# Dealing 256 KB of a weight matrix to the eight lower DMA engines of a load-bound decode kernel

## Chip, cores and metric

One core of one Trainium2 chip. The metric is the device time of one execution, in microseconds (us). The profile is one execution recorded by the hardware profiler; its span is some 2 us shorter than the time of the same execution (658.6 against 660.69 for the kernel before).

## The reference

```python
xn = _layernorm(x)                      # x: 2 x 1 x 512, bf16
q  = (xn @ wq) -> 2 x 32 x 1 x 128
scores = q k_cache^T * 128**-0.5        # k_cache, v_cache: 2 x 32 x 8192 x 128
attention = softmax(scores) @ v_cache -> @ wo      # wo: 4096 x 512
mlp = relu(xn @ w1) @ w2                # w1: 512 x 1792, w2: 1792 x 512
return x + attention + mlp
```

Nearly all of the 280.5 MB that are read are keys and values. w2, which the change touches, is 1.8 MB.

## The kernel before

SyncE issues every large load into one queue, in the order in which the data is needed: wq, w1, w2, then key and value tiles of 4 MB, at the end wo in five pieces. A 128-partition load is carried by all sixteen DMA engines (the trace has sixteen landings for each), so each load is complete only when its slowest engine is. w2 goes 14 rows of 1 KB to a partition:

```python
w2_sb = w_sb[:, KT*Dff : KT*Dff + FT*D].rearrange("p (j n) -> p j n", j=FT)   # FT = 14
...
@(lambda f: f(nc.sync))
def _(sp):
    sp.dma_start(w1_sb, B_w1.rearrange("(p kt) f -> p kt f", kt=KT)).then_inc(dW1, 16)
    sp.dma_start(w2_sb, B_w2.rearrange("(p j) n -> p j n", j=FT)).then_inc(dW2, 16)
    load_k(0); load_k(1); load_v(0)
    for t in range(NP - 2):                   # NP = 32 pairs of heads
        sp.wait_ge(pT[NG - 1], t + 1);  load_k(t + R)
        sp.wait_ge(sW, t + 1);          load_v(t + 1)
    ...                                       # last values in two halves
    for c in range(NC):                       # wo, cuts (0, 14, 21, 27, 30, 32)
        sp.dma_start(wo_sb[:, sl, :], wo_v[:, sl, :]).then_inc(dW[c], 16)
```

TensorE does the MLP while the first keys are on their way, and then loops over the pairs:

```python
    for j in range(FT):                       # 14 x 4 products of w1
        for kt in range(KT): pe.matmul(hp[:, j, :], lhsT=w1_v[:, kt, j, :], rhs=xz[...], ...)
    ...
    pe.wait_ge(sF, 2); pe.wait_ge(dW2, 16)    # ReLU done (VectorE), w2 landed
    for j in range(FT):                       # 14 products of w2
        pe.matmul(y, lhsT=hT[:, j, :], rhs=w2_sb[:, j, :], ...)
    ...
    with pe.Fori(16, 16 * (NP // R) + 1, 16) as n16:      # 16 turns of R = 2 pairs
        for r in range(R): pe.reg_add(reg, reg, 1); step(r, reg, n16)
```

## Time and profile before

| | before |
|---|---|
| time, 3 runs | 660.98, 663.39, 1773.56 us (median 663.39) |
| profiled execution | 660.69 us, span 658.6 |
| DMA engines busy with data (mean of sixteen) | 99.2% of the span |
| TensorE busy | 85% |
| last piece of wo lands on eight engines / on the other eight | 653.04 to 653.44 / 654.67 to 654.85 us |

The last row says that half of the engines finish 1.4 us later than the other half, although nothing shows that they carry more bytes: the 128 packets of w2 (0.537 us each) land on all sixteen within 0.38 us, which is less than one packet.

Two groups of instructions show which side waits for which. In a line of this view stand the source line, the engine, what is done, the count, then busy time and mean ns of one, then the engine's idle time just before these instructions and what ended it.

```profile
L285 PE MATMUL tp<-identb,ks 128*128 128x128 bf16 x4096 | 323.5, 229 | 68.4 <-DMA ks<-in_A_k_cache_dram 68.4
...
L305 PE MATMUL ot<-prm,vs 128*128 128x64 bf16 x4224 | 156.1, 192 | 4.2 <-issue 4.2
```

TensorE idles 68.4 us ahead of the transposes of keys, all of it for key loads; "issue" (time in which the profile shows nothing that the engine waited for) is 4.2 us ahead of the value products.

The packets show directly what makes an engine late. The first of the instruction blocks (nine packets of 16 KB, on a queue of their own) runs from 29.574 to 30.634 us. Two engines end a data packet at 29.578. Behind one of them the data goes on at once; behind the other the next data packet begins only at 30.620 and takes 1.68 us, where the others take 1.21.

### The profile page before, as it was taken

How to read it: one execution, taken by the hardware profiler on the slowest of the kernel's cores; microseconds unless marked ns; L12 is line 12 of the kernel's file. 1: busy time of each engine (PE TensorE's matmuls, PEld its weight loads, DVE VectorE, ACT ScalarE, POOL GpSimd, SP SyncE). 2: the span in 40 equal slices, each digit the busy share in tenths (PEclk: the TensorE clock that was granted, in tenths of full speed). 3: DMA queues.
4: the chain of work that ended last, by engine and by line, in shares of the span. 5: the costliest groups of instructions: out<-in, count | busy, mean ns of one | idle time of the engine just before them, and what ended most of it. 6: DMA issues, size and time to landing. Idle time of an engine off the chain costs nothing.

```text
span 658.6 us, 26859 instructions
## 1 busy us (share of the span) xinstructions
PE 559.9 (85%) x12737; PEld 535.1 (81%) x12737; DVE 253.2 (38%) x436; ACT 255.8 (39%) x403; POOL 9.0 (1%) x46
## 2 busy tenths in 40 slices
PE   2998799987989878879887887997878997887896
PEld 0488798987879878879887887987878987887895
DVE  1144344442434433334443343443434443333441
ACT  1043444443433434334353434344333444333340
POOL 1000000000000000000000000000000000000000
PEclk9799999998998988999898899898989998898988
DMA  8999999999999999999999999999999999999996
GB/s 365 430 444 418 439 430 429 432 428 442 422 442 424 436 428 432 432 428 444 420 442 428 432 430 430 434 430 442 424 436 428 432 432 428 440 424 442 426 424 281
DMA packets 10542, 280.66 MB, mean 426 GB/s; under 512 B 1186, under 2 KB 1188, under 8 KB 1700
## 3 DMA queue, kind: packets, MB, share of 16 engines
q1 hardware_dynamic: 10528, 280.50, 99.2%
q8 instruction: 9, 0.15, 0.1%
q14 instruction: 1, 0.01, 0.0%
q10 hardware_dynamic: 4, 0.00, 0.0%
HBM read 280.50 MB, written 0.00 MB: 426 GB/s over the span
## 4 chain that ended last, share of the span: by engine, by line
DMA 58%; PE 37%; ACT 2%; issue 1%; SPq 1%; ACTq 0%; DVE 0%
DMA ks<-in_A_k_cache_dram 54%; PE tp L285 21%; PE Sc L292 11%; PE ot L305 4%; DMA w_sb<-in_A_wo_dram 4%; ACT kT L412 2%; ACT L412 1%; SPq L187 0%; PE Sc L340 0%; SPq L182 0%; PE Sc L343 0%; SPq L170 0%; SPq L169 0%; SPq L163 0%; PE ot L397 0%
## 5 line engine op out<-in xcount | busy, mean ns | idle before, releaser
L285 PE MATMUL tp<-identb,ks 128*128 128x128 bf16 x4096 | 323.5, 229 | 68.4 <-DMA ks<-in_A_k_cache_dram 68.4
L412 DVE COPY kT<-tp 128x1024 bf16<-128x1024 bf16 x320 | 219.7, 691 | 324.3 <-PE tp L285 324.2
L285 PEld LDWEIGHTS tp<-identb,ks 128*128 128x128 bf16 x4096 | 254.8, 102 | 72.3 <-DMA ks<-in_A_k_cache_dram 72.2
L412 ACT COPY kT<-tp 128x1024 bf16<-128x1024 bf16 x192 | 194.3, 1012 | 233.4 <-PE tp L285 233.3
L292 PE MATMUL Sc<-q,kT 128*128 128x64 bf16 x4096 | 216.8, 196 | 7.6 <-ACT kT L412 5.7
L292 PEld LDWEIGHTS Sc<-q,kT 128*128 128x128 bf16 x4096 | 178.4, 100 | 11.3 <-ACT kT L412 9.0
L305 PE MATMUL ot<-prm,vs 128*128 128x64 bf16 x4224 | 156.1, 192 | 4.2 <-issue 4.2
L305 PEld LDWEIGHTS ot<-prm,vs 128*128 128x128 bf16 x4224 | 139.0, 97 | 7.0 <-issue 4.4
L525 ACT COPY nm<-Sc 128x2 f32<-128x2 f32 x32 | 5.1, 160 | 118.5 <-PE Sc L343 118.5
L529 ACT ACTIVATE prm<-Sc,nm 64x128 bf16<-64x128 f32 x64 | 25.7, 401 | 4.3
L466 DVE TENSOR_REDUCE mcol<-Sc 64x1 bf16<-64x128 f32 x64 | 18.6, 290 | 18.7 <-PE Sc L292 18.3
L412 ACT ACT_TABLE_LOAD x16 | 20.5, 1283 | 2.2
L240 PE MATMUL ot<-vs,xz 128*16 128x512 bf16 x32 | 9.5, 470 | 8.6 <-DMA vs<-in_A_wq_dram 8.6
L517 ACT COPY OTf<-ot 128x2 f32 x32 | 5.1, 160 | 26.9 <-PE ot L305 26.9
L471 DVE TENSOR_REDUCE mx<-Sc 1x2 bf16<-1x128 bf16 x32 | 8.9, 278 | 16.9 <-PE Sc L340 16.9
L240 PEld LDWEIGHTS ot<-vs,xz 128*16 128x16 bf16 x32 | 3.3, 105 | 14.4 <-issue 12.2
L225 POOL COPY q<-qb 128x2 bf16<-128x2 bf16 x32 | 5.8, 184 | 588.9 <-PE Sc L292 566.1
L529 ACT ACTIVATION_READ_ACCUMULATOR prm<-Sc,nm x64 | 11.8, 185 | 0.0
L442 DVE TENSOR_SCALAR qs<-ot 16x512 bf16<-16x512 f32 x1 | 0.7, 679 | 18.0 <-PE ot L240 18.0
L340 PE MATMUL Sc<-identb,mcol 128*1 128x128 bf16 x32 | 7.0, 217 | 0.0
L270 PE MATMUL Sc<-w_sb,hT 128*2 128x512 bf16 x14 | 5.8, 604 | 0.1
L343 PE MATMUL Sc<-mx,onesb 1*128 1x2 bf16 x32 | 5.5, 172 | 0.0
(56 smaller groups left out, 37.5 us busy)
## 6 DMA issues: line engine op xcount, KB each, us to landing
ks<-in_A_k_cache_dram SPq DMA_DIRECT2D x32, 4096.0 KB, 26.7
vs<-in_A_v_cache_dram SPq DMA_DIRECT2D x31, 4096.0 KB, 31.3
vs<-in_A_wq_dram SPq DMA_DIRECT2D x1, 4096.0 KB, 12.1
vs<-in_A_v_cache_dram SPq DMA_DIRECT2D x2, 2048.0 KB, 19.3
w_sb<-in_B_w_dram SPq DMA_DIRECT2D x2, 1792.0 KB, 17.9
w_sb<-in_A_wo_dram SPq DMA_DIRECT2D x1, 1792.0 KB, 25.4
w_sb<-in_A_wo_dram SPq DMA_DIRECT2D x1, 896.0 KB, 27.1
w_sb<-in_A_wo_dram SPq DMA_DIRECT2D x1, 768.0 KB, 28.5
```

Of the source, the lines that this page charges most:

```text
L225: g.tensor_copy(q2[t % R][:], qb[:, 2 * t:2 * t + 2]).then_inc(sQ1, 1)
L240: i = pe.matmul(qp, lhsT=xz[:, kt, Z - g * Bsz:Z - g * Bsz + QG * Bsz], rhs=vs[1][:, (kt * QG + g) * 512:(kt * QG + g + 1) * 512], start=( ...
L270: i = pe.matmul(y, lhsT=hT[:, j, :], rhs=w2_sb[:, j, :], start=(j == 0), stop=(j == FT - 1),)
L285: t = pe.transpose(tp[e % 4][:, i, :], ks[r][:, kk * Dh:(kk + 1) * Dh], identb[:])
L292: t = pe.matmul(Sc[r][:, 2 * kk:2 * kk + 2 * REP], lhsT=kT[e % 4][:, i, :], rhs=rep(q2[r][:]), start=True, stop=True,)
L305: t = pe.matmul(ot[r][:, 0:2 * REP], lhsT=vs[r][:, kk * Dh:(kk + 1) * Dh], rhs=rep(prm[r][:, kk, :]), start=(kk == 0), stop=(kk == KB - 1),)
L340: pe.transpose(tr_of(r), mcol[r][:], identb[:]).then_inc(sT, 1)
L343: pe.matmul(bc_of(r), lhsT=onesb[:], rhs=mx[r][:], start=True, stop=True).then_inc(sB, 1)
L412: fn(kT[e % 4][:], tp[e % 4][:]).then_inc(kR[e], 1)
L466: m = v.tensor_reduce(out=mcol[i][half, :], in_=S_of(i)[half, :, u], axis=AX.X, op=ALU.max)
L471: v.tensor_reduce(out=mx[i][:], in_=tr_of(i).rearrange("o (u m) -> o u m", u=2), axis=AX.X, op=ALU.max, negate=True,).then_inc(sX, 1)
L529: x = a.activation(out=prm[i][half, :, u], in_=S_of(i)[half, :, u], func=ACTF.Exp, bias=nm[i][half, u:u + 1], scale=1.0, accum_out=RS[half ...
```

## The change

The intent: give every partition 12 rows of w2 in one load, and send the other 256 rows, 4 to a partition, to the lower 64 partitions only. They come in eight loads of 8 rows. Each takes every fourth partition, p, p+4 ... p+28. That such a load goes to a fixed half of the DMA engines was my assumption; the trace of after bears it out (64 landings for the eight loads, and two clusters in the first keys, below). I call the eight that take the small loads the lower ones, engines 0 to 7, and the others the upper ones, 8 to 15; these are names, for the trace has no numbers. An upper engine then carries 16 KB less (eight packets of 12 KB in place of 14), a lower one 16 KB more (the same, and eight of 4 KB). The MLP's products follow the new layout. Cut to its core:

```diff
+    FA = FT - 2               # 12 rows on all partitions
+    FB = 2 * (FT - FA)        # 4 more on the lower 64
+    FJ = FA + FB              # 16
...
-        sp.dma_start(w2_sb, B_w2.rearrange("(p j) n -> p j n", j=FT)).then_inc(dW2, 16)
+        sp.dma_start(
+            w2_sb[:, 0:FA, :], B_w2[0:P * FA, :].rearrange("(p j) n -> p j n", j=FA)
+        ).then_inc(dW2, 16)
+        w2_v = B_w2[P * FA:, :].rearrange("(p j) n -> p j n", j=FB)
+        for p in (0, 1, 2, 3, 32, 33, 34, 35):
+            sl = slice(p, p + 29, 4)
+            sp.dma_start(w2_sb[sl, FA:FA + FB, :], w2_v[sl]).then_inc(dW2b, 16)
...
-        for j in range(FT):
+        for j in range(FJ):                       # products of w1: 48 + 16 of half width
             for kt in range(KT):
                 i = pe.matmul(
-                    hp[:, j, :],
-                    lhsT=w1_v[:, kt, j, :],
+                    hp[0:HP if j >= FA else P, j, :],
+                    lhsT=w1_b[:, kt, j - FA, :] if j >= FA else w1_a[:, kt, j, :],
...
+        pe.wait_ge(dW2b, 16 * 8)
-        for j in range(FT):
+        for j in range(FJ):                       # 12 products of w2, and 4 over 64 partitions
...
-        v.tensor_scalar(out=hT[:], in0=hp, ..., op0=ALU.max).then_inc(sF, 1)
+        for sl in (slice(0, P), slice(0, FA)), (slice(0, HP), slice(FA, FJ)):
+            t = v.tensor_scalar(out=hT[sl], in0=hp[sl], ..., op0=ALU.max)
+        t.then_inc(sF, 1)
```

## The prediction

> **What bounds the kernel now.** I read the page first: busy shares, the queue lines, then the chain that ended last.

> ```profile
> span 658.6 us, 26859 instructions
> ...
> DMA  8999999999999999999999999999999999999996
> ...
> q1 hardware_dynamic: 10528, 280.50, 99.2%
> q8 instruction: 9, 0.15, 0.1%
> ...
> DMA 58%; PE 37%; ACT 2%; issue 1%; SPq 1%; ACTq 0%; DVE 0%
> ```

> The transfers are the bound: the data queue's packets fill 99.2% of sixteen DMA engines' span, while TensorE, the busiest compute engine, is at 85%. The next question is whether the queue ever runs dry. The view by stretch of time says no: the DMA share (the column before GB/s) is 1.00 in every stretch until the last loads.

> ```profile
> 2.00:33.00 31.00, 19.51 (x114) 8.94 (x115) 3.62 (x9) 2.46 (x4) 2.22 (x9) 0.89 1.00 421
> 33.00:159.00 126.00, 110.68 (x2702) 107.31 (x2698) 53.84 (x92) 54.95 (x87) 1.29 (x7) 1.00 1.01 432
> 159.00:623.00 464.00, 401.99 (x9264) 392.49 (x9264) 185.69 (x312) 190.42 (x299) 4.24 (x23) 0.94 1.00 432
> ```

> So the end is set by bytes per DMA engine plus whatever else an engine is made to do. The chain of waits, in order of time, shows how it closes: the output weights' last piece lands, then a short tail.

> ```profile
> 625.73 29.12 DMA w_sb<-in_A_wo_dram
> 654.85 0.05 issue
> 654.90 0.39 PE ot L397 x8
> ```

> A load is complete when its last engine is, so I read the sixteen landings of every load in the trace one by one. w2 lands between 21.28 and 21.66 us, all sixteen within 0.38. The first key tile already has one straggler: fifteen between 31.01 and 31.39, one at 32.73. In the tile that lands from 108.70 on, seven are late; the last piece of wo lands on eight engines at 653.04 to 653.44 and on eight at 654.67 to 654.85. The cause stands in the packets of the queue named "instruction": seven 16 KB blocks between 29.57 and 107.2 us and one at 650.36 (the ninth, at 654.27, comes too late to matter), 1.07 us each on average. After every one of them exactly one more engine is about 1.3 us late and stays so. No engine is hit twice before the end. The kernel therefore ends some 1.4 us after its eight unhindered engines are done (654.85 against 653.44), with no difference in the bytes they carry.

> [...]

> **The change part by part.** Its only aim can be that deal: 256 KB of w2 (64 partitions x 4 rows x 1 KB) ride on engines 0 to 7, and engines 8 to 15 are relieved of 2 rows in each of 8 partitions, 16 KB.

> Upper engines: w2's 14336-byte packets take 0.537 us each, 8 of them 4.29 (first landings of w1 and w2 are 17.00 and 21.28, which agrees). With 12 rows I estimate 12/14 x 0.537 = 0.460, times 8 = 3.68: 0.61 us less.

> Lower engines: the same 3.68, plus eight 4 KB packets. From 3072 bytes in 0.122 us and 6144 in 0.241 I put 4 KB at 0.161, plus 0.009 for each load's semaphore write: 8 x 0.170 = 1.36. In all 5.04 against 4.29: 0.75 us more.

> If the eight late engines are the upper ones, their last landing goes from 654.85 to 654.24, and the lower ones' from 653.44 to 654.19: evened out almost exactly, 0.6 us gained. That is all there is to win here.

> Beside that, SyncE issues eight more loads ahead of the first keys. The two neighbours take 0.42 us to issue, so the first key tile is issued about 8 x 0.47 = 3.8 us later, near 6.1 us. The queue then holds work until 21 us: hidden.

> TensorE and VectorE pay too:

> ```profile
> 22.70 3.52 PE L253 MATMUL ot<-xz,w_sb 128*128 128x2 bf16 x56
> ...
> 26.26 0.19 DVE L446 TENSOR_SCALAR hT<-ot 128x28 bf16<-128x28 f32 x1 [2.77 <-PE ot L253]
> ...
> 26.50 5.84 PE L270 MATMUL Sc<-w_sb,hT 128*2 128x512 bf16 x14
> ...
> 32.77 1.51 PE L285 MATMUL tp<-identb,ks 128*128 128x128 bf16 x24 [0.43 <-DMA ks<-in_A_k_cache_dram]
> ```

> 56 products of w1 become 48 plus 16 of half width: at 3.52/56 = 0.063 us each, 8 more are 0.50. The second ReLU adds about 0.2. w2's 14 products become 16; they follow each other every 0.43 us, so 0.85 more. w2 has landed by about 22.8 on the slower engines, before this block needs it. Sum 1.55 us, less the 0.43 of waiting in the last line: TensorE starts on the first keys 1.1 us later. Does that starve the queue? I took, for each load, its time of issue against the first landing of the load before it. The smallest margin in the loop is 5.3 us (the key tile issued at 83.61; what stood before it began to land at 89.28), and 15 to 20 us after 190 us, once TensorE waits for keys. So 1.1 us is swallowed, and a change that lengthens a compute chain still costs nothing.

> Sum on the path to the end: 0.6 us less of 658.6, 0.1%.

> **The rivals.** First, the late engines are not the upper ones. The refills take a new engine each time, which looks like going round in order, but nothing in this trace says where the round begins. If one late engine is among the lower eight, the end moves from 654.85 to about 655.6, +0.75 us. For it: the lack of engine numbers. Against it: the change only makes sense if its author saw the slack in the lower half[...]. I give the intended half 2 in 3.

> Second, refills move. [...] One more block in the loop, or another round, puts 1.3 us on an engine that now has no slack: then the end is 0.7 us later in place of 0.6 earlier. [...]

> Third, eight small loads are dearer than their packets, through a gap between loads. The last pieces of wo (2 KB packets) took 0.65 us for eight with one semaphore write, which is 8 x 0.081: no gap to be seen. Even 0.1 us each would be 0.8 us more on engines that had 1.4 of slack.

> Fourth, the later start of TensorE or a late issue lets the queue run dry. The margins of 5.3 us and 15 us speak against it; it would take over 4 us of delay to show.

> **Range and chances.** Every path is within about 1.5 us, 0.2%. What decides the figure is the scatter of runs: before gives 660.98 and 663.39, the profiled run 660.69, and one run of 1773.56 which no structure here explains and which a median of three would normally drop. The mean of the three ordinary ones is 661.7; less 0.6 is about 661.1, and with a third for the rivals I say 661.2. For 8 in 10 I take 659.4 to 663.8, which is this scatter and a little for another chip. Over 2% (13 us) is out of reach either way except by a run that is disturbed: 0.01 each.

> **What would show it.** In the changed kernel's trace: 64 packets of 4 KB near 0.16 us and 128 of 12 KB near 0.46; w2's upper part landing near 20.7 and the last small load near 22.1; the first keys' products starting near 34; key and value tiles still landing every 9.71 us; and the last piece of wo landing with its sixteen engines within about 0.6 us, not 1.8, at about 654.2. Wrong would be: two groups of landings still 1.8 us apart or more (the wrong half was relieved), ten or more instruction packets before the end, or a DMA share below 1.00 in a stretch of the loop.

What is cut at the marks is what no run shows. 4.29 - 3.68 = 0.61 us less for an upper engine, 5.04 - 4.29 = 0.75 us more for a lower one, so 0.6 us less at the end. That loads of 8 rows ride on the lower half was an assumption.

## The result, and the profile after

| | before | after |
|---|---|---|
| time, median of 6 runs each | 661.35 (660.80 to 1773.56) | 661.39 (661.32 to 661.54) |
| span of the profiled execution | 658.6 | 659.3 |
| last piece of wo, first and last engine | 653.04, 654.85 | 652.68, 655.54 |

The ratio, after over before, is 0.9998 with a 95% interval of 0.9983 to 1.0013. It and every ratio below is the mean time of one kernel's runs over that of the other's of the same rounds, so it is not quite the ratio of the medians that I quote. Executions over 1.5% slower than the fastest of the same kernel are left out of the means. Here the runs of before scatter more (660.80 to 661.71, and 663.39) than the question is wide, so "same" is clear and the sign is not. Repeated with five rounds (below), the change was 0.3 us slower in the median, and every run of it lay above all nine of before.

The page of the kernel after. The row of DMA tenths and the line of the instruction queue are letter for letter those shown of before: full from start to end, nine instruction blocks.

```profile
span 659.3 us, 26888 instructions
...
q1 hardware_dynamic: 10656, 280.50, 99.1%
...
DMA 56%; PE 39%; ACT 2%; issue 1%; SPq 0%; DVE 0%; ACTq 0%
```

128 more packets (10656 against 10528) are in the data queue, and the same bytes. The last line, the chain that ended last by engine, is the same mix as before. By stretches (busy time of PE, PEld, DVE, ACT, POOL, then TensorE's granted clock, the DMA share and GB/s):

```profile
33.00:159.00 126.00, 114.92 (x2703) 111.83 (x2702) 54.73 (x92) 54.95 (x87) 1.31 (x7) 0.96 1.00 429
159.00:623.00 464.00, 400.83 (x9264) 391.15 (x9264) 185.56 (x312) 190.56 (x300) 4.29 (x23) 0.94 1.00 432
```

The share stays 1.00, so the queue never ran dry, and the loop moves the same 432 GB/s. Only the end differs. In the chain, in order of time:

```profile
625.89 29.65 DMA w_sb<-in_A_wo_dram
655.54 0.05 issue
655.58 0.39 PE ot L412 x8
```

The last landing is 0.69 us later than before's 654.85, and the chain behind it is unchanged in kind. To see why, the sixteen landings of some loads, read one by one from the trace (us; in brackets how many engines):

```
load                before                               after
w2, large part      21.28 to 21.66 (16)                  20.59 to 21.23 (16)
w2, small, last     -                                    22.40 to 22.93 (8)
first keys          31.01-31.39 (15), 32.73 (1)          30.42-30.94 (7), 31.60-32.08 (8), 32.20 (1)
last piece of wo    653.04-653.44 (8), 654.67-654.85 (8) 652.68, 652.89 (2), 653.61-654.26 (12), 655.34, 655.54 (2)
```

Each of the eight small loads landed on eight engines (64 landings for the eight, in 64 packets of 4 KB). The row of the first keys shows the intended deal at work. Seven engines are 0.45 to 0.6 us earlier than before, eight are some 0.6 to 0.7 later; one, already hit by an instruction block, is on 32.20 where it was on 32.73, so it is one of the relieved (upper) half. The last row is the count that the prediction lacked. Had all eight late engines been upper ones, there would be sixteen landings together near 654.2. Instead there are two in front (upper, relieved, never hit), twelve in the middle, and two 1.1 to 1.3 us behind these. The two behind can only be engines that carry more *and* were hit: lower ones. Twelve in the middle are then six upper hit ones and six lower unhit ones. **Of the eight late engines, six were upper and two lower.**

The compute part of the new kernel, from the view in order of time (start, duration, engine, line, work):

```profile
2.36 5.48 SPq L182 DMA_DIRECT2D w_sb<-in_B_w_dram  x8
7.88 0.92 SPq L163 DMA_DIRECT2D ks<-in_A_k_cache_dram  x2
...
22.66 4.06 PE L266 MATMUL ot<-xz,w_sb 128*128 128x2 bf16 x64
...
26.76 0.25 DVE L462 TENSOR_SCALAR hT<-ot 128x24 bf16<-128x24 f32 x2 [3.31 <-PE ot L266]
...
27.06 5.96 PE L285 MATMUL Sc<-w_sb,hT 128*2 128x512 bf16 x16
...
32.95 1.51 PE L300 MATMUL tp<-identb,ks 128*128 128x128 bf16 x24
```

w1's products take 4.06 us where they took 3.52, w2's 5.96 where they took 5.84, and the first keys' transposes begin at 32.95 instead of 32.77. The eight small loads occupy SyncE for 5.48 us (0.62 to 0.80 each), so the first keys are issued at 7.88. Both are early enough: in the loop the smallest margin between the end of the issue of a load and the first landing of the one before it fell from 5.34 to 3.72 us, and stayed positive.

### The profile page after: what moved, and what is told of

Its sections match the earlier page's. It is cut to its first block, busy times and chain, and to the rows that moved or that the text cites. A ratio compares the mean times of both kernels' runs of the same rounds, so it can differ in the third digit from the quotient of the medians.

```text
span 659.3 us, 26888 instructions
## 1 busy us (share of the span) xinstructions
PE 562.9 (85%) x12747; PEld 538.3 (82%) x12747; DVE 253.4 (38%) x437; ACT 255.9 (39%) x403; POOL 9.0 (1%) x46
## 2 busy tenths in 40 slices
DMA  8999999999999999999999999999999999999996
## 3 DMA queue, kind: packets, MB, share of 16 engines
q1 hardware_dynamic: 10656, 280.50, 99.1%
HBM read 280.50 MB, written 0.00 MB: 425 GB/s over the span
## 4 chain that ended last, share of the span: by engine, by line
DMA 56%; PE 39%; ACT 2%; issue 1%; SPq 0%; DVE 0%; ACTq 0%
DMA ks<-in_A_k_cache_dram 50%; PE tp L300 21%; PE Sc L307 11%; DMA w_sb<-in_A_wo_dram 4%; PE ot L320 4%; DMA vs<-in_A_wq_dram 2%; ACT kT L427 2%; PE ot L252 1%; PE Sc L285 1%; PE ot L266 1%; ACT L427 1%; SPq L199 0%; PE Sc L355 0%; PE Sc L358 0%; SPq L194 0%
## 5 line engine op out<-in xcount | busy, mean ns | idle before, releaser
L285 PE MATMUL Sc<-w_sb,hT 128*2 128x512 bf16 (+1 forms) x16 | 6.0, 544 | 0.1
```

The source lines that it names most:

```text
L285: i = pe.matmul(y, lhsT=hT[half, j, :], rhs=w2_sb[half, j, :], start=(j == 0), stop=(j == FJ - 1),)
```

## The experiments

The theory after the result (T): the byte arithmetic per engine is right; the time moved up because two of the eight engines that lose time to instruction blocks are lower ones, to which the change gave more bytes. Rivals: the extra compute (R1), the small loads costing more than their packets (R2), the instruction blocks having moved to other engines by the change itself (R3), and total bytes rather than an engine's bytes setting the end (R4). "Before" is always the kernel before on the same chip: 660.82 (660.69 to 661.02), 660.90 (660.83 to 661.05), 660.85 (660.70 to 662.03).

### Which engines are late? Marks in the queue

The trace has no engine numbers, so I name engines by small loads, marks, of k rows each, k from 1 to 15. The fifteen marks of the wider kind below made 120 packets and 120 landings, which is 1 + 2 + ... + 15. I assumed that the engines of a smaller mark are always among those of the next larger one, and that those of the mark of 8 rows are the lower half. Then each engine holds a different number of marks, and engine e is the name of the one with 15 - e; from there on they arrive in that order: 15 first, then 14, 13 and so on. Two measurements fit this: the first places in the list of landings of the marked kernel before are 0.14 to 0.15 us apart (a 4 KB packet takes 0.159 in after), and the order of halves is the one of the unmarked kernel (end of this section). The first two attempts, on before and on after, used 1792-byte rows.

```diff
+        for k in range(1, 16):                       # ahead of the first key load
+            sp.dma_start(mk[0:k, (k - 1) * 896:k * 896], wo_r[0:k, 0:896]).then_inc(dM, 16)
```

> The kernel before, with fifteen small loads of 1 to 15 rows (1792 bytes a row, into spare space) put between w2 and the first keys, so that DMA engine e gets 15-e small packets and the engines can be told apart in the trace. Right result. Theory (each 16 KB instruction block puts one engine about 1.35 us behind, whichever half it is in): seven engines are hit between 29 and 107 us, no one twice, and they are a mix of both halves; from the changed kernel's landings I expect the order upper, upper, upper, lower, lower, upper, upper, with an eighth, upper, at 650 us. Rival (the upper eight are the slow ones, as the prediction hoped): all hits in engines 8 to 15.

> The changed kernel with the same fifteen marking loads. Right result. Theory: the same engines are hit in the same order as in the marked kernel before, because the round of the instruction blocks starts at a fixed engine and the program is only 22 TensorE instructions longer; two of the seven are in the lower half and end last, about 3 us after the first engine. Rival (which engines are hit is chance of the run or of the program's length): another set or another order.

663.54 and 665.94 us. Inconclusive. The small loads left gaps of 0.1 to 1.1 us on engines, and the packets of one engine could not all be followed through them. Only the first hit in before could be followed: an engine with 3 marks, which is engine 12; in after, one of the upper half. So the marks were made wider, 4 KB a row, and laid in partitions of their own:

```diff
+        at = 0
+        for k in range(1, 16):
+            sp.dma_start(mk[at:at + k, :], wo_r[0:k, 0:2048]).then_inc(dM, 16)
+            at += k
```

> As the first marked run of the kernel before, but with 4 KB rows: the 1792-byte loads left gaps in the queue in which the engines could not be followed. Engine e now gets 15-e packets of 0.16 us, so that engine 0 is 2.5 us behind engine 15 and the landings name the engines. Right result. The unrolled run has shown that a ninth block hits an engine for the second time, so the theory is now: eight engines take the blocks in turn, and they are of both halves. Expected: seven single hits of 1.35 us between 29 and 108 us, some on low engines (late landings) and some on high ones. Rival: all eight in the upper half; then no landing below the middle of the list moves.

> The same marks in the changed kernel. Theory: the same eight engines in the same order as in the marked kernel before; from the unmarked trace two of the first seven are lower. Rival: the set or the order is another in each kernel or each load of a program (the first marked run seemed to begin with a low engine, the changed kernel with an upper one), so that no fixed deal can fit it.

664.11 and 664.86 us. Now the engines arrive spread out, and a hit one steps back by about 1.3 to 1.7 us in the list of landings. (Followed packet by packet in the marked kernel before, six hit engines step back by 1.53 to 1.56 us.) On before, the first keys land at 33.04 and then 0.14, 0.29 and 0.66 us after it: engines 15, 14 and 13 stand with 0, 1 and 2 marks, the engine with 3 is missing from its place at about 0.45 and found further back. It is engine 12, and it took the first block. Two blocks later the entries 0.14 and 0.29 have gone and two at 1.83 and 1.84 have come: engines 14 and 13. The other five were an engine at 1.40, one at 1.65, one at 1.02, one at 1.24 and one at 0.66. By place in the list these are two of the lower half, then two that fit 9 and 10, and 11. On after: engine 12 first, 14 and 13 next, two of the lower half (fitting 5 and 6), then 9, 10 and 11. **The same eight, in the same order: 12, 14 and 13, two lower ones, 9, 10, 11.** By these names engines 11 to 14 are exact; 5, 6, 9 and 10 are read off places between neighbours and may be off by one. One thing in the trace of after stays unexplained: near 52 us an engine in front, 15 by its first packets, also lost about 0.4 us, without a block of its own. The list agrees with the count of two lower and six upper from the unmarked kernel after, and with the order there, as far as the tiles separate it: the engines in front fall from seven to five by 49.85 us (three upper ones hit), single landings at 62.58 and then 72.29 and 72.46 are lower ones, and the front has four left at 69.39, three at 79.11 and two at 652.68 (three more upper ones). And it refutes R3: the change did not move the blocks. That it was so in before already is what the prediction could not see.

### Do the blocks go round all sixteen engines?

If the round has only eight stations, a ninth block hits an engine a second time. Doubling the loop body of TensorE brings more blocks:

```diff
-        with pe.Fori(16, 16 * (NP // R) + 1, 16) as n16:
-            for r in range(R):
+        n16 = nc.alloc_register(mybir.EngineType.PE, "landed");  pe.reg_mov(n16, 0)
+        with pe.Fori(0, NP // (2 * R)):
+            for r in range(2 * R):
                 pe.reg_add(reg, reg, 1)
-                step(r, reg, n16)
+                if r % R == 0: pe.reg_add(n16, n16, 16)
+                step(r % R, reg, n16)
```

> The kernel before with four pairs in one turn of TensorE's loop in place of two: the same work and bytes, but a loop of about 3100 TensorE instructions[...]. Right result. Theory (instruction blocks put engines behind): [...] the last piece of wo lands 7 to 8 us later, near 662, time near 669 (ratio 1.011 to 1.013).[...] Rival (blocks are hidden, the late engines late for another reason): no change of time whatever the count of blocks.

The terms of its 7 to 8 us, a count of blocks times the 1.35 us that one puts an engine behind (32.73 against 31.39 us in the first keys of before), are cut: the count rested on what no run shows. The run counted 113.

724.57 us (719.0 to 728.36), ratio 1.0936 (1.0893 to 1.098): slower by far more than any theory said. The page shows why:

```profile
span 726.2 us, 26844 instructions
...
DMA  8999999699979999799997999979997999969892
...
q1 hardware_dynamic: 10528, 280.50, 91.0%
q8 instruction: 113, 1.85, 1.1%
...
PE 73%; issue 18%; ACT 5%; DMA 4%; SPq 0%; DVE 0%; ACTq 0%
...
L285 PE MATMUL tp<-identb,ks 128*128 128x128 bf16 x4096 | 327.2, 228 | 71.0 <-issue 69.2
...
L305 PE MATMUL ot<-prm,vs 128*128 128x64 bf16 x4224 | 167.9, 196 | 49.2 <-issue 49.2
```

### Does an engine's byte count set the end?

e12 adds 96 KB to each lower engine on top of the change, in six loads of 8 rows, in partitions spaced as in the change; the wait on the data is off the path.

```diff
+        for p in (0, 1, 2, 3, 32, 33):
+            sl = slice(p, p + 29, 4)
+            sp.dma_start(mk[sl, :], wo_r[sl, 0:8192]).then_inc(dM, 16)
```

> The first run with more loads on the lower engines was spoilt: 32 loads of 0.67 us each on SyncE let the queue of the upper engines run dry until 24 us. Here 96 KB more on each of engines 0 to 7 come in six 8-row loads of 16 KB a row[...], behind the changed kernel's eight. Right result. Theory (the end is that of two lower engines that a block has hit): 6 x 0.625 = 3.75 us later than the changed kernel, last piece of wo near 659.2, time near 665.0. Rival (only the total counts): 768 KB at 432 GB/s, 1.8 us later, 663.1.

665.24 us (665.15 to 665.31), ratio 1.0062 (1.0047 to 1.0078); last landings 658.60, then two engines at 659.23 and 659.24. Both numbers are on the forecast of T (665.0 and 659.2) and away from R4's 663.1. The shift against after, 659.24 - 655.54 = 3.70 us, is the time of the six added packets (0.615 us for one of 16 KB, the median in before), and the two hit lower engines are still the last pair. The queue stayed full, and its last landing still ends the kernel:

```profile
q1 hardware_dynamic: 10752, 281.29, 98.9%
...
630.47 28.77 DMA w_sb<-in_A_wo_dram
659.24 0.05 issue
```

An earlier, worse version of this run put the extra bytes in 24 more small loads:

```diff
+        for c in range(3):
+            for p in (0, 1, 2, 3, 32, 33, 34, 35):
+                sl = slice(p, p + 29, 4)
+                sp.dma_start(mk[sl, c], w2_v[sl]).then_inc(dM, 16)
```

> The changed kernel with its eight small loads made four times (three more copies go to spare space): 96 KB more on each of engines 0 to 7, nothing on the others. Right result. Theory (the end is that of the engine with most bytes and a refill, a lower one): 24 x 0.17 = 4.1 us later than the changed kernel, last piece of wo near 659.6 us, time near 665.5. Rival (bytes count, wherever they go): 768 KB at 432 GB/s, 1.8 us later, 663.2. Second rival (queue order swallows it): no change, 661.4.

666.04 us (665.77 to 666.21), ratio 1.0078 (1.0062 to 1.0095), near T's number for a reason that is not T's. In order of time:

```profile
7.87 15.94 SPq L188 DMA_DIRECT2D mk<-in_B_w_dram  x24
23.85 0.91 SPq L165 DMA_DIRECT2D ks<-in_A_k_cache_dram  x2
```

SyncE spends 15.94 us on issuing 24 small loads, 0.66 each. The first keys are issued at 23.85. By then the upper engines have long finished their part of w2 (landed by 21.12), and no packet of the keys begins before 25.03: half of the queue ran dry, and all sixteen engines land the first keys late, fourteen of them from 35.5 to 36.5. The agreement of the total is a coincidence, and the run proves nothing about bytes. It does show what the change's eight loads would cost if there were not 21 us of work queued ahead of them.

Being small is not what makes these loads slow to issue. The fifteen marks of 1 to 15 neighbouring rows, in the marked kernel before, took 0.24 to 0.39 us each, the one of 8 rows 0.32:

```profile
2.34 5.34 SPq L176 DMA_DIRECT2D mk<-in_A_wo_dram  x15
```

The loads of the change, 8 rows that lie four partitions apart, took 0.62 to 0.80; those of 128 rows in before took 0.33 to 0.53. That the distance of the rows is the cause is not shown separately.

### Is it the extra compute, or the small loads?

e8 is before with the change's compute alone: 8 more w1 products, a second ReLU, 2 more w2 products, into buffers that nobody reads.

```diff
+        for j in range(2):
+            for kt in range(KT): pe.matmul(hp_all[0:HP, FT + j, :], lhsT=w1_x[:, kt, j, :], ...)
+        for j in range(2): pe.matmul(Sc[0][0:Bsz, :], lhsT=hX[0:HP, j, :], rhs=w2_sb[0:HP, j, :], ...)
+        v.tensor_scalar(out=hX[0:HP], in0=hp_all[0:HP, FT:FT + 2, :], ..., op0=ALU.max)
```

> The kernel before, its loads untouched, with the changed kernel's extra compute: 8 more products of w1 at half width, a second ReLU, 2 more products of w2 over 64 partitions, whose results nobody uses. Right result. Theory (all of the change in time comes from the deal of bytes[...]): time of the kernel before within 0.15 us, last piece of wo at 654.9. Rival (the longer compute, or the shifted instruction blocks, are what made the changed kernel 0.3 us slower than before): 0.3 us or more above before.

660.79 us (660.64 to 661.01), ratio 0.9995 (0.9981 to 1.0008); last landings in the two groups of before, 653.05 to 653.48 and 654.51 to 655.02. The extra compute is free, and R1 falls.

e3 is after with the eight small loads made into one 64-partition load. I expected it to spread the 256 rows evenly over sixteen engines (my assumption, not shown here) and so to land where before does; a saving of seven loads would have favoured R2.

```diff
-        for p in (0, 1, 2, 3, 32, 33, 34, 35):
-            sl = slice(p, p + 29, 4)
-            sp.dma_start(w2_sb[sl, FA:FA + FB, :], w2_v[sl]).then_inc(dW2b, 16)
+        sp.dma_start(w2_sb[0:HP, FA:FA + FB, :], w2_v).then_inc(dW2b, 16)
```

> The changed kernel with its eight 8-row loads made as one load of 64 rows[...]: same layout of w2, same work on TensorE and VectorE, no uneven deal. Right result. Theory (the uneven deal loads late engines of the lower half further): landings of one spread of about 1.8 us as in the kernel before, last piece of wo at 654.9, time equal to the kernel before within 0.1 us and 0.5 to 0.7 below the changed kernel. Rival (the layout or the 1.1 us of added compute is what made the changed kernel end later): time as the changed kernel's.

661.84 us (661.74 to 662.27), ratio 1.0015 (1.0001 to 1.0029): a miss, and apart from e9 the slowest of the variants of the same bytes. The 4 KB packets, 0.159 us in after, took 0.248 us in the mean here and up to 0.411, and all of the first keys land about 1.07 us late (32.08 against 31.01). Busy time hides it. The stretch from 20 to 25 us, first of after, then of e3, in the columns used above:

```profile
20.00:25.00 5.00, 5.00 (x52) 3.31 (x51) 0.68 (x1) 0.00 (x0) 0.00 (x0) 0.98 1.05 447
```

```profile
20.00:25.00 5.00, 5.00 (x58) 3.49 (x56) 0.68 (x1) 0.00 (x0) 0.00 (x0) 1.00 1.10 394
```

The DMA share is full in both (this view books a whole packet where it begins, hence values above 1), and e3 moves 394 GB/s in place of 447. With each packet cut at the borders, the two us from 21 to 23 show it more sharply: a share of 1.01 in both, 428 GB/s in after and 271 in e3. Equally busy, fewer bytes: these packets are slower, not more. What slows them is not shown; the marks, loads of 1 to 15 neighbouring rows, took 0.16 to 0.37 us for 4 KB. It speaks for cutting the rows into loads of 8 rows four partitions apart, as the change does (0.159 us). In after the last small load lands at 22.93, 0.8 us later than the prediction's 22.1, but the first keys' lower engines are only 0.6 to 0.7 us later than before, as the byte sum says. R2 is small at most.

### Is the change slower at all?

The kernel after, unchanged, with five rounds:

> The changed kernel once more, beside the others on one chip. Theory: 0.5 to 0.7 us (0.1%) above the kernel before, last piece of wo landing in two or three groups over some 2.9 us. Rival (no difference at all, the 0.7 us of the two profiles is chance): interval of the ratio centred on 1.0000.

661.22 us (661.15 to 661.46), ratio 1.0006 (0.9992 to 1.0019). The interval contains 1, but the five runs lie all above the nine of before, by 0.3 us in the median, less than the 0.5 to 0.7 expected. The last piece of wo lands in the same 2, 12, 2: 652.72 and 652.96, then twelve from 653.72 to 654.43, then 655.30 and 655.37.

### Relieving the true late engines

Since most late engines are upper ones and engines 0 to 3 were never hit in the marked runs, wo's last row could go to the latter alone, in one load of 124 rows and one of 4. The trace of e16 has eight landings for the two, which I read as four engines for each; that these are engines 0 to 3 is my assumption. As a control, e15 cuts wo's last piece in two in the ordinary way (cuts 30, 31, 32); e16 sends its last row so:

```diff
-    cuts = (0, 14, 21, 27, 30, WJ)
+    cuts = (0, 14, 21, 27, 30, 31, WJ)                   # e15 and e16
...
-            sp.dma_start(wo_sb[:, sl, :], wo_v[:, sl, :]).then_inc(dW[c], 16)
+            for pp in (slice(0, P),) if c < NC - 1 else (slice(0, 124), slice(124, P)):
+                sp.dma_start(wo_sb[pp, sl, :], wo_v[pp, sl, :]).then_inc(dW[c], 16)   # e16 only
```

> Control for the next run: the kernel before with the last piece of wo, 2 rows a partition, cut into two of 1 row, all sixteen engines as ever. Right result. Theory: the last landing is where it was, 654.85, or 0.05 to 0.1 later for the smaller packets, and the tail after it is up to 0.15 shorter: time of the kernel before within 0.15 us. Rival: more pieces cost 0.3 us or more.

660.85 us (660.76 to 661.03), ratio 0.9997 (0.9983 to 1.001): the cut costs nothing.

> The kernel before, the last row of wo (128 KB) loaded by engines 0 to 3 alone, in two loads of 124 and of 4 rows[...]. The marked runs say that these four, with 4, 7, 8 and 15, are never hit by an instruction block. Right result. Theory: the hit engines are relieved of 8 packets of 1 KB, 0.35 us; engines 0 to 3 carry 32 of about 0.048 us, 1.55 us, in the 1.4 us that they had to spare; the last landing comes 0.2 to 0.3 us earlier than in the control, time 0.2 to 0.3 us below it. Rival (the marks misled me and one of the four is hit[...]): 0.8 us or more above the control.

661.04 us (660.89 to 661.11), ratio 0.9998 (0.9985 to 1.0012), 0.2 us above the control where I expected 0.2 to 0.3 below: a miss. The row before the last landed up to 655.24 (control 654.67), and the piece before that is already late in the chain:

```profile
625.62 29.33 DMA w_sb<-in_A_wo_dram
654.96 0.05 issue
655.00 0.71 PE ot L398 x20
```

The packets are slower here: 1 KB packets went from 46 ns to 54.7 in the mean, up to 108. What was taken off the late engines' byte counts came back as time, by my reading in these slower packets; what slows them is not shown. No kernel is clearly faster than before.

## Why the prediction was right and where it was wrong

**The range and the verdict were right; the direction, by the landings and the repeat, was not.** 661.2 was predicted, 661.39 measured, inside 659.4 to 663.8, and within 2%. But the range is 4.4 us wide, for a gain of 0.6: it would have held the loss as well, and so proves nothing about the deal. That the figure itself came so close is luck. It took 661.7 for the kernel before, a mean raised by the one run of 663.39, where nearly all later runs lie near 660.9, and then took off 0.6 us that did not come. The reading that the end is set by the bytes of an engine plus the blocks it is made to fetch held: the queue stayed at a share of 1.00, and e12 put 3.70 us on the end with bytes on the lower engines alone.

**The byte steps were right.** w2's large part now follows w1 by 20.59 - 16.91 = 3.68 us, as predicted; 12 KB packets take 0.460 us (predicted 0.460), 4 KB ones 0.159 (0.161). In the first keys the lower engines are 0.6 to 0.7 us later, against 0.75.

**The step that failed** is "If the eight late engines are the upper ones, their last landing goes from 654.85 to 654.24 ... evened out", and with it the sum "0.6 us less". I gave the intended half 2 in 3 because the change would make no sense otherwise, which is an argument about the author and not about the chip. Only six of the eight are upper. The first rival's number, 654.85 + 0.75 = 655.6, is what came: 655.54, and 655.37 in the repeat. As there are two lower engines among the late ones and a load waits for its slowest, what the six gained counts for nothing. The change in time is smaller than that of the landing: +0.3 us in the repeat for +0.52 of landing. The landing is compared with the first profile of before, though; e8, which loads as before does, landed last at 655.02 and not at 654.85, so some 0.2 us of it may be scatter, and the runs do not say more.

**A size inside that step:** "1.3 us" for a block is the distance between the two groups of landings. The engine itself is set back by about 1.5 us (1.53 to 1.56 for six engines, above).

**A wrong picture inside that step:** "The refills take a new engine each time, which looks like going round in order". They do go to a new engine each time, but the round has eight engines, and the eighth block ends it (e9). A round of sixteen was never in play.

**Smaller misses, all hidden.** Compute: w1's 0.5 us came, but w2's two more products cost 0.12 us instead of 0.85, because the four over 64 partitions began 0.31 us and then 0.22 us after one another instead of 0.43; the keys start at 32.95, not 34, and e8, which starts the keys at 33.58 and so 0.8 us later than before, is no slower for it. Issue: 0.47 us was estimated for each small load, 0.62 to 0.80 was measured, and the first keys are issued at 7.88 instead of 6.1. The margin held.

**The other rivals.** The block count did not move (nine in both), a gap between small loads is at most small, and the queue did not run dry.

**What stays open.** Why just these eight engines take the blocks; the exact numbers of four of them; what made 663.39 and 1773.56 in the first runs of before; why the packets of e3 and e16 are slower; and whether rows dealt only to the engines never hit, in packets of the usual speed, would gain. By the arithmetic here that would be worth some 0.7 us, half of the 1.4 us between the two groups, 0.1%.

## What to carry to other kernels

When a queue is full from start to end, read the landings of the last load engine by engine, for the end belonged here to the engines with the most bytes and an instruction block on top (655.34 and 655.54 us in after, 659.23 and 659.24 in e12), and moving bytes helps only if you know which engine that is: mark them before you deal. Look at the time of a packet after dealing, since the runs whose packets became slower (4 KB in 0.248 us against 0.159 in e3, 1 KB in 54.7 ns against 46 in e16) gained nothing. And count what a load costs to issue in just the form that you use (0.32 us for 8 neighbouring rows, 0.62 for 8 rows four partitions apart), and what a longer loop body of TensorE costs (113 blocks in place of nine, and 9% of the time, in e9), before using either as a harmless probe.
